# Moving the low part of h ahead of ez on GpSimd, and taking v's low weights last

## The chip, the cores and the metric

The kernel runs on one core of a Trainium2 chip, as one launch. The time is the device time of an execution in microseconds (us); lower is better. A core has a TensorE (PE; its weight loads are shown as PEld), a VectorE (DVE), a ScalarE (ACT), a GpSimd (POOL) and a SyncE (SP) that here only starts DMAs. Each engine works through its own list of instructions in order, and waits on semaphores for the others.

## The reference

Two blocks follow each other on x of 2048 tokens by 512 channels, in float32:

```python
h  = x + attention(layernorm(x))       # 32 heads of 16, linear attention
h2 = h + mixer(layernorm(h))           # MLP over the tokens, F = 1792
```

In the attention, q, k and v come from one product with `wqkv`. Each head's q and k go through a small product with `w_phi` and two softmaxes, of the logits and of their negatives; these are the features phi. With them `kv = phi_k^T v` and `z = sum phi_k` over all tokens, and the output is `phi_q kv / (phi_q z + 1e-6)`, times `wo`. The mixer normalises h per token, multiplies `w1` (2048 x 1792) over the token axis, adds `b1`, takes a tanh-gelu, multiplies `w2` (1792 x 2048) and adds `b2`.

## The kernel before

The tokens are cut into 16 tiles of 128 (`NT`). Every large product is made in three passes: each operand is split in a rounded high part and the low part that is left, and TensorE adds high x high, high x low and low x high in PSUM (`mm3`, lines 63 to 67). `split` (line 58) makes the two parts: ScalarE copies the high one (line 60), and another engine subtracts to get the low one (line 61).

**Preparation (lines 223 to 362).** The weights of q, k and v come in 12 chunks (0 to 3 q, 4 to 7 k, 8 to 11 v). They are centred (`center`), folded with w_phi or transposed on TensorE into PSUM (`fold`), and from there ScalarE writes the high parts (`hi_w`, line 285) and VectorE subtracts the low ones (`lo_w`, line 289). Chunks 10 and 11 of v lie in the two buffers of the PSUM pool `ps_v`; v's first product `v0` (line 335) takes the buffer that chunk 10 held. `proj` (lines 122 to 135) makes one product of a tile with 512 columns: 4 contraction steps of 3 matmuls. Its `by_part` form, used once for k's first tile, orders them by part of the weights instead. From line 294 on the order of TensorE, VectorE, ScalarE and GpSimd is written out by hand.

**k and v for all tiles, and q for six (lines 401 to 421).** Here the order on the engines is not written out; a planner that works on its own estimates of durations orders it when the kernel is built, and steps of this loop can also come between those written by hand. For each tile: k's product and its logits on VectorE, the exponential on ScalarE, the normalisation on GpSimd (`k_norm`), v's product; `kv` collects phi_k^T v in PSUM.

**Attention (lines 423 to 702).** From line 424 the order on the four engines is again written by hand. zB, the sum z spread over all partitions (lines 490 to 494), is copied by ScalarE from a product on TensorE, and starts GpSimd's work of this part. Then the loop `for it in range(NT + 4)` (line 648) works on several tiles at once, each at another step:

- `s_pq(it + 1)`: GpSimd multiplies a tile of features with its weights w (line 465);
- `s_num`, `s_ol`: the numerators of two tiles, every second iteration;
- `s_den`: VectorE's chain that starts with the sums of ez (line 456) and ends with w (line 462);
- `s_ez(it + 3)`: GpSimd multiplies a tile of exponentials with zB (line 447); `negate()` makes the negated logits there (lines 164 and 165);
- `fills(it)`: the first products of the mixer, for two column blocks of w1, block 0 with h tile it - 5 and block 1 with h tile it - 6. One such `fill` is six matmuls: for each half of the columns, high weights x high h (line 65), high weights x low h (line 66), low weights x high h (line 67);
- `q_exp`: an exponential of q on ScalarE (line 176), until iteration 7;
- `s_hn(it - 4)`: the normalised h tile, from r2 that GpSimd made with `s_rstd` (line 590) in the iteration before: three steps on ScalarE (lines 593, 595, 60) and the low part on GpSimd (line 61, shown as hs);
- `s_wo`, `s_tr`, `s_h`, `s_moments`: the product with wo, transposes, h itself and its statistics.

The weights of the mixer come in pairs of row tiles (`stream`, `fill_load`): a DMA, the high part on ScalarE (line 614), and later the low part on VectorE (`flush`, line 606). Pair 2 (rows of tiles 2 and 3) of block 0 is loaded at the end of iteration 5, its low part subtracted in iteration 6 and used in iteration 7; pair 2 of block 1 comes an iteration later each time.

**The rest of the mixer (lines 704 to 911)**: the remaining column blocks, gelu, and the second product (lines 823, 824 and 827). The change does not touch it.

Of the kernel before, what the change touches and what calls it, by code (L numbers as in the profile page):

```python
# [20 lines left out]
KD = D // P  # L21
# [15 lines left out]
def block_kernel(ctx: ExitStack, tc: tile.TileContext, x, xT, wT, phic, wo, w1, b1, w2, b2,  # L37
# [25 lines left out]
    def mm3(o, ah, al, bh, bl, first, last):  # L63

        nc.tensor.matmul(o, ah, bh, start=first, stop=False)  # L65
        nc.tensor.matmul(o, ah, bl, start=False, stop=False)  # L66
        nc.tensor.matmul(o, al, bh, start=False, stop=last)  # L67
# [22 lines left out]
    wvh = wp.tile([P, KD, D], F32R, name="wvh")  # L90
    wvl = wp.tile([P, KD, D], F32R, name="wvl")
    zacc = wp.tile([P, NG, P], F32, name="zacc")
    ps_k = a1.enter_context(tc.tile_pool(name="ps_k", bufs=2, space=PSUM))
    ps_v = a1.enter_context(tc.tile_pool(name="ps_v", bufs=2, space=PSUM))
# [24 lines left out]
        nc.vector.tensor_scalar(ve, st[:, 1:2], 1.0 / D, EPS, op0=ALU.mult, op1=ALU.add)  # L119
        nc.gpsimd.tensor_tensor(r1[:, t:t + 1], ve, mhalf[:, :1], op=ALU.pow)  # L120

    def proj(t, wh, wl, pool, name, by_part=False):
        o = pool.tile([P, D], F32, name=name, tag=name)
        if by_part:
            half, whole = [slice(0, D // 2), slice(D // 2, D)], slice(0, D)
            turn = [(0, wh, half[0]), (0, wh, half[1]), (1, wh, whole), (0, wl, half[0]), (0, wl, half[1])]
            for i, (a, w, cols) in enumerate(turn):
                for kt in range(KD):
                    nc.tensor.matmul(o[:, cols], X[t][:, a, kt, :], w[:, kt, cols], start=i == 0 and kt == 0,
                                     stop=i >= 3 and kt == KD - 1, skip_group_check=True)  # L130
            return o
        for kt in range(KD):
            mm3(o, X[t][:, 0, kt, :], X[t][:, 1, kt, :], wh[:, kt, :], wl[:, kt, :],
                kt == 0, kt == KD - 1)
        return o
# [39 lines left out]
    def exps(t, e):  # L175
        nc.scalar.activation(e, e, AF.Exp, scale=r1[:, t:t + 1])
# [46 lines left out]
    with tc.tile_pool(name="prep", bufs=1) as prep:  # L223
        pc = prep.tile([P, 72], F32, name="pc")
        ph = prep.tile([P, 4, P], F32, name="ph")
        WR = {}

        def load_w(c):
            if c % 2 == 0:
                pair = big.tile([P, 2, D], F32, name="wraw2", tag="big")  # L230
                WR[c], WR[c + 1] = pair[:, 0], pair[:, 1]
            nc.sync.dma_start(WR[c], wT[c * P:(c + 1) * P, :])

        nc.scalar.dma_start(pc, phic)
        for c in range(4, 8):
            load_w(c)
        xr = {0: load_x(0), 1: load_x(1)}
        nc.sync.dma_start(ident, ident_in)
        for c in range(8, 12):
            load_w(c)  # L240
        xr[2] = load_x(2)
        load_h(0)
        load_h(1)
        xr[3] = load_x(3)
        for c in range(4):
            load_w(c)
        load_h(2)
        xr[4] = load_x(4)
        load_h(3)
        nc.sync.dma_start(mask, kvmask)  # L250
        nc.sync.dma_start(b1s, b1)
        nc.sync.dma_start(b2s, b2)

        FO = {}
        HL = {0: (wqh, wql), 1: (wkh, wkl), 2: (wvh, wvl)}

        def center(c, vector):

            mu = prep.tile([P, 1], F32, name="mu", bufs=3)
            if vector:  # L260
                nc.vector.reduce_sum(mu, WR[c], axis=AX.X)
                nc.vector.tensor_scalar_mul(mu, mu, -1.0 / D)
                nc.vector.tensor_scalar(WR[c], WR[c], mu, None, op0=ALU.add)
            else:
                junk = prep.tile([P, D], F32, name="junk")
                nc.scalar.activation(junk, WR[c], AF.Copy, scale=-1.0 / D, accum_out=mu)
                nc.scalar.activation(WR[c], WR[c], AF.Identity, bias=mu)

        def fold(c, pool, name):
            FO[c] = pool.tile([P, KD, P], F32, name=name, tag=name)  # L270
            for kt in range(KD):
                if c < 8:
                    nc.tensor.matmul(FO[c][:, kt, :], WR[c][:, kt * P:(kt + 1) * P], ph[:, c % 4, :],
                                     start=True, stop=True)
                else:
                    nc.tensor.transpose(FO[c][:, kt, :], WR[c][:, kt * P:(kt + 1) * P], ident)

        def parts(c):
            return [w[:, :, c % 4 * P:(c % 4 + 1) * P] for w in HL[c // 4]]

        def hi_w(c, vector=False):
            if vector:
                nc.vector.tensor_copy(parts(c)[0], FO[c])
            else:
                nc.scalar.activation(parts(c)[0], FO[c], AF.Copy)

        def lo_w(c):
            hi, lo = parts(c)
            nc.vector.tensor_sub(lo, FO[c], hi)

        warm = ps_k.tile([P, P], F32, name="pk_ps", tag="pk_ps")
        for _ in range(WARM):
            nc.tensor.matmul(warm, ones, ones, start=True, stop=True)
        with tc.manual_schedule(engines={ET.PE, ET.DVE, ET.Activation, ET.Pool}):

            nc.gpsimd.tensor_mul(ph.rearrange("p c (a f) -> p c a f", f=DH),
                                 pc[:, 0:64].rearrange("p (c f) -> p c f", f=DH).unsqueeze(2).to_broadcast([P, 4, 8, DH]),
                                 pc[:, 64:72].unsqueeze(1).unsqueeze(3).to_broadcast([P, 4, 8, DH]))
            center(4, True)
            center(5, False)  # L300
            fold(4, ps_q, "pu")
            center(6, True)
            fold(5, ps_q, "pu")
            center(7, False)
            fold(6, ps_v, "pv")
            fold(7, ps_v, "pv")
            hi_w(4, True)
            hi_w(5, True)
            hi_w(6, True)
            split_x(0, xr[0])  # L310
            hi_w(7)
            for c in range(4, 8):
                lo_w(c)
            split_x(1, xr[1])
            k0 = proj(0, wkh, wkl, ps_k, "pk_ps", True)
            center(8, True)
            for c in range(9, 12):
                center(c, False)
            k1 = proj(1, wkh, wkl, ps_k, "pk_ps")
            for c in range(8, 12):  # L320
                fold(c, *((ps_q, "pu"), (ps_v, "pv"))[c // 10])
            k_ops(0, k0)
            split_x(2, xr[2])
            k_ops(1, k1)
            stats_x(0)
            k2 = proj(2, wkh, wkl, ps_k, "pk_ps")
            for c in range(8, 12):
                hi_w(c)
            for c in range(8, 12):
                lo_w(c)  # L330
            stats_x(1)
            exps(0, PK[0])
            split_x(3, xr[3])
            split_x(4, xr[4])
            v0 = proj(0, wvh, wvl, ps_v, "pv")
            k_ops(2, k2)
            stats_x(2)
            k3 = proj(3, wkh, wkl, ps_k, "pk_ps")
            k_norm(0)
            center(0, True)  # L340
            v_out(0, v0)
            exps(1, PK[1])
            center(1, False)
            exps(2, PK[2])
            v1 = proj(1, wvh, wvl, ps_v, "pv")
            k_ops(3, k3)
            fold(0, ps_q, "pu")
            fold(1, ps_q, "pu")
            k_norm(1)
            center(2, False)  # L350
            v_out(1, v1)
            hi_w(0)
            hi_w(1)
            lo_w(0)
            lo_w(1)
            center(3, False)
        stats_x(3)
        exps(3, PK[3])
        for c in range(2, 4):
            fold(c, ps_q, "pu")  # L360
            hi_w(c)
            lo_w(c)
# [208 lines left out]
    def s_x(t):  # L571
        HT[t] = ak.tile([P, D], F32, name="h", bufs=4)
        nc.sync.dma_start(HT[t], x[t * P:(t + 1) * P, :])
# [18 lines left out]
    def s_hn(t):  # L592
        nc.scalar.activation(VE[t][:, 1:2], VE[t][:, 1:2], AF.Copy, scale=r2[:, t:t + 1])
        hn = ak.tile([P, D], F32, name="hn")
        nc.scalar.activation(hn, HT[t], AF.Identity, scale=r2[:, t:t + 1], bias=VE[t][:, 1:2])
        HN[t] = big.tile([P, 2, D], F32R, name="hs", tag="big")
        split(HN[t][:, 0], HN[t][:, 1], hn, nc.gpsimd)
# [50 lines left out]
    for it in range(NT + 4):  # L648
        even = it % 2 == 0
# [15 lines left out]
            den = den[1:]  # L665
        if it < NT:
            s_x(it)
        if it + 3 < NT:
            s_ez(it + 3)
        negate()  # L670
# [1 line left out]
        fills(it)  # L672
        q_exp(0)
        logits = q_logits(1)
        if it >= 4 and even:
            s_hn(it - 4)
        if 3 <= it < NT + 3 and even:
            s_moments(it - 3)
        if it > 1 and even and it - 2 < NT:
# [161 lines left out]
    for n, (sp, p) in enumerate(STEPS):  # L841
        t = 2 * sp
# [5 lines left out]
        if p == 0:  # L848
            bank = []
            for _ in range(6):  # L850
                pool = (ps_f, ps_q, ps_b, ps_b)[n_bank % 8 // 2]
# [109 lines left out]
```

## Time and profile before

| what | value |
|---|---|
| time, median of 3 runs | 524.17 us (523.75 to 524.24) |
| the profiled execution's own time | 524.12 us |
| its span in the trace | 522.3 us |
| TensorE busy | 516.6 us, 99% |
| VectorE / ScalarE / GpSimd busy | 386.5 / 282.3 / 239.8 us |
| HBM traffic | 46.81 MB read, 11.14 MB written |

A row of the timeline gives start and duration in us, the engine, the line of the kernel, the operation, what it writes and reads by the program's names, the shapes, and a count of merged instructions; in brackets stands how long the engine was idle before it and what ended that. The rows of the sums by stretch give busy time (and number of instructions) of PE, PEld, DVE, ACT and POOL, the clock that TensorE was granted (1.00 is full), and what the DMA engines did. A waits row gives the total, the number of times and the longest one.

### The profile page before, as it was taken

The page shows a single profiled execution, that of the slowest core. Times are in us where ns is not written, and L with a number is a line of the kernel's source. Part 1 is how long each engine was busy: PE and PEld are TensorE (multiplying, and loading weights), DVE is VectorE, ACT ScalarE, POOL GpSimd, SP SyncE. Part 2 cuts the span into 40 slices and gives each one's busy share as a digit, 9 for nine tenths or more (in the row PEclk, how much of TensorE's full clock was granted, in tenths as well). Part 3 has the DMA queues.
Part 4 walks back from the last instruction along what each step waited for, and adds up shares of the span by engine and source line. Part 5 has one row for each costly group of instructions (what it writes and reads, how often), then busy time and mean ns, then how long its engine had stood idle before and what let it go on. Part 6 is the DMA issues. An engine that isn't in the chain of part 4 may idle for free.

```text
span 522.3 us, 8917 instructions
## 1 busy us (share of the span) xinstructions
PE 516.6 (99%) x3379; PEld 436.5 (84%) x3379; DVE 386.5 (74%) x681; ACT 282.3 (54%) x496; POOL 239.8 (46%) x188
## 2 busy tenths in 40 slices
PE   9999999999999999999999999999999999999997
PEld 8788888887877767888788888888899999999997
DVE  6893999986899998863227424725779888988985
ACT  6999853424246876666956423625453434434430
POOL 2579799985999999874424000000002112212220
PEclk9999999999999999999999999999999999999999
DMA  8544210020131324343333354532215687678734
GB/s 317 198 122 122 80 43 22 1 80 24 30 113 60 102 86 136 105 130 130 102 100 102 102 179 143 176 92 77 76 45 115 158 191 161 120 164 186 163 43 82
DMA packets 36298, 58.52 MB, mean 112 GB/s; under 512 B 3744, under 2 KB 19360, under 8 KB 36256
## 3 DMA queue, kind: packets, MB, share of 16 engines
q1 hardware_dynamic: 31936, 51.37, 31.2%
q0 software_dynamic: 4032, 6.42, 9.1%
q8 instruction: 26, 0.43, 0.3%
q10 hardware_dynamic: 288, 0.17, 0.1%
q14 instruction: 16, 0.13, 0.1%
HBM read 46.81 MB, written 11.14 MB: 111 GB/s over the span
## 4 chain that ended last, share of the span: by engine, by line
PE 90%; POOL 7%; DVE 2%; issue 1%; ACT 0%; POOLq 0%
PE pu L65 12%; PE pu L66 12%; PE pu L67 11%; PE py L823 11%; PE py L827 10%; PE py L824 6%; PE pv L66 3%; PE pv L67 3%; PE pv L65 3%; PE pk_ps L65 2%; PE pk_ps L67 2%; PE pk_ps L66 2%; POOL ez L447 2%; POOL eq L465 2%; PE po L67 2%; PE po L65 2%
## 5 line engine op out<-in xcount | busy, mean ns | idle before, releaser
L66 PE MATMUL pu<-hs,whi 128*128 128x512 f32 x224 | 87.6, 391 | 1.2 <-POOL hs L61 1.2
L65 PE MATMUL pu<-hs,whi 128*128 128x512 f32 x224 | 87.4, 395 | 0.0
L67 PE MATMUL pu<-hs,wlo 128*128 128x512 f32 x224 | 87.0, 389 | 0.0
L606 DVE TENSOR_TENSOR wlo<-wraw,whi 128x512 fp32r<-128x512 f32 x56 | 43.8, 784 | 53.2 <-ACT whi L614 53.0
L882 POOL DMA_DIRECT2D out<-ot x7 | 6.2, 887 | 153.9 <-DVE ot L878 153.9
L796 ACT ACTIVATE whi<-wraw 128x1792 fp32r<-128x1792 f32 x28 | 47.4, 1701 | 46.7 <-PE py L823 20.6
L805 DVE TENSOR_TENSOR wlo<-wraw,whi 128x1792 fp32r<-128x1792 f32 x28 | 56.5, 2022 | 12.1 <-PE py L824 8.9
L823 PE MATMUL py<-uf,whi 128*128 128x512 f32 x175 | 63.4, 399 | 0.0
L614 ACT ACTIVATE whi<-wraw 128x512 fp32r<-128x512 f32 x56 | 34.9, 627 | 49.6 <-PE pu L66 45.3
L65 PEld LDWEIGHTS pu<-hs,whi 128*128 128x128 f32 x224 | 42.1, 188 | 10.9 <-issue 2.5
L66 PEld LDWEIGHTS pu<-hs,whi 128*128 128x128 f32 x224 | 42.1, 188 | 10.4 <-POOL hs L61 2.1
L67 PEld LDWEIGHTS pu<-hs,wlo 128*128 128x128 f32 x224 | 42.1, 188 | 8.6
L824 PE MATMUL py<-uf,wlo 128*128 128x256 f32 x175 | 49.2, 281 | 0.0
L447 POOL TENSOR_TENSOR ez<-eq,zB 128x1024 f32<-128x1024 f32 x16 | 38.4, 2400 | 4.4 <-ACT zB L494 4.4
L827 PE MATMUL py<-uf,whi 128*128 128x256 f32 x210 | 39.0, 283 | 0.0
L823 PEld LDWEIGHTS py<-uf,whi 128*128 128x128 f32 x175 | 33.0, 188 | 6.8
L200 POOL TENSOR_TENSOR pk<-pk,sk 128x1024 f32<-128x1024 f32 x16 | 31.0, 1940 | 7.6 <-DVE sk L199 5.0
L534 ACT ACTIVATE pht<-tn 128x512 f32<-128x512 f32 x32 | 17.4, 596 | 30.2 <-PE tn L532 30.2
L827 PEld LDWEIGHTS py<-uf,whi 128*128 128x128 f32 x210 | 32.4, 189 | 1.4
L824 PEld LDWEIGHTS py<-uf,wlo 128*128 128x128 f32 x175 | 33.1, 189 | 0.0
L465 POOL TENSOR_TENSOR eq<-eq,w 128x1024 f32<-128x1024 f32 x16 | 32.3, 2017 | 1.3 <-DVE w L462 1.2
L61 POOL TENSOR_TENSOR hs<-hn,hs 128x512 fp32r<-128x512 f32 x16 | 21.6, 1350 | 23.7 <-ACT hs L60 23.7
(179 smaller groups left out, 1344.2 us busy)
## 6 DMA issues: line engine op xcount, KB each, us to landing
wraw<-in_w SPq DMA_DIRECT2D x56, 256.0 KB, 2.8
wraw<-in_w SPq DMA_DIRECT2D x28, 512.0 KB, 4.1
xraw<-in_xT SPq DMA_DIRECT2D x16, 256.0 KB, 2.8
xh<-in_x SPq DMA_DIRECT2D x16, 256.0 KB, 2.6
h<-in_x SPq DMA_DIRECT2D x16, 256.0 KB, 2.7
out<-h SPq DMA_DIRECT2D x16, 256.0 KB, 2.4
out<-ot POOLq DMA_DIRECT2D x14, 256.0 KB, 4.8
wraw<-in_wT SPq DMA_DIRECT2D x12, 256.0 KB, 4.4
```

Source lines behind the costliest of these rows:

```text
L65: nc.tensor.matmul(o, ah, bh, start=first, stop=False)
L66: nc.tensor.matmul(o, ah, bl, start=False, stop=False)
L67: nc.tensor.matmul(o, al, bh, start=False, stop=last)
L447: nc.gpsimd.tensor_mul(EZ[t], EQ[t], zB)
L465: nc.gpsimd.tensor_mul(heads(EQ[t]), heads(EQ[t]), W[t].rearrange("p g c h -> p (g c h)").unsqueeze(2).to_broadcast([P, 2 * H, DH]))
L606: LO.append(nc.vector.tensor_sub(wl_, raw, wh_).ins)
L614: nc.scalar.activation(wh_, raw, AF.Copy)
L796: nc.scalar.activation(WH[g], RAW[g], AF.Copy)
L805: nc.vector.tensor_sub(wl_, RAW[g], WH[g])
L823: nc.tensor.matmul(o, a[0], b, start=start, stop=stop, skip_group_check=True)
L824: nc.tensor.matmul(o[:, 0], a[1], b[:, 0], start=False, stop=stop, skip_group_check=True)
L827: nc.tensor.matmul(o[:, half], a[x], b[:, y], start=start and first and i == 0, stop=stop and i == 2, skip_group_check=True)
```

## The change

It has two parts. In the preparation, v's first product goes through the four contraction steps with high x by high weights, then low x by high weights, then high x by low weights; and VectorE subtracts the low parts of v's weight chunks in the order 10, 11, 8, 9. In the attention loop, `s_hn(it - 4)` of the even iterations from 4 on stands ahead of `s_ez(it + 3)`, instead of behind `q_logits`. On GpSimd it thus passes ez and the first `negate()`, on ScalarE what `fills` may issue there and the exponential of `q_exp`. The odd iterations stay as they are.

```diff
-    def proj(t, wh, wl, pool, name, by_part=False):
+    def proj(t, wh, wl, pool, name, by_part=False, low_last=False):
         o = pool.tile([P, D], F32, name=name, tag=name)
-        if by_part:
+        if by_part or low_last:
             half, whole = [slice(0, D // 2), slice(D // 2, D)], slice(0, D)
             turn = [(0, wh, half[0]), (0, wh, half[1]), (1, wh, whole), (0, wl, half[0]), (0, wl, half[1])]
+            if low_last:
+                turn = [(0, wh, whole), (1, wh, whole), (0, wl, whole)]
             for i, (a, w, cols) in enumerate(turn):
                 for kt in range(KD):
                     nc.tensor.matmul(o[:, cols], X[t][:, a, kt, :], w[:, kt, cols], start=i == 0 and kt == 0,
-                                     stop=i >= 3 and kt == KD - 1, skip_group_check=True)
+                                     stop=w is wl and kt == KD - 1, skip_group_check=True)
             return o
...
-            for c in range(8, 12):
+            for c in (10, 11, 8, 9):
                 lo_w(c)
...
-            v0 = proj(0, wvh, wvl, ps_v, "pv")
+            v0 = proj(0, wvh, wvl, ps_v, "pv", low_last=True)
...
         if it < NT:
             s_x(it)
+        if it >= 4 and even:
+            s_hn(it - 4)
         if it + 3 < NT:
             s_ez(it + 3)
         negate()
...
         logits = q_logits(1)
-        if it >= 4 and even:
-            s_hn(it - 4)
         if 3 <= it < NT + 3 and even:
```

## The prediction

> **What bounds the kernel now.** The order of reading is: the page's busy times, the sums by stretch, the waits, then the timeline at the places that these name. The first row below is the page's, the others are sums by stretch: between 23.3 us and the end TensorE is busy without a break, except between 172 and 190 us.
>
> ```profile
> PE 516.6 (99%) x3379; PEld 436.5 (84%) x3379; DVE 386.5 (74%) x681; ACT 282.3 (54%) x496; POOL 239.8 (46%) x188
> ```
> ```profile
> 23.30:172.00 148.70, 148.70 (x1214) 121.81 (x1213) 127.63 (x229) 86.32 (x154) 129.72 (x89) 1.00 0.22 67
> ...
> 190.00:519.00 329.00, 329.00 (x1937) 282.59 (x1934) 222.54 (x380) 163.10 (x277) 84.50 (x75) 1.00 0.48 122
> ```
>
> So a microsecond is won only where TensorE stands still, and lost wherever a new wait stops it. Next come the view of waits and TensorE's timeline at the one stop of size after the warm-up.
>
> ```profile
> PE pu L66 <- POOL hs L61: 1.2, 1, 1.2
> ```
> ```profile
> 186.68 0.39 PE L67 MATMUL pu<-hs,wlo 128*128 128x512 f32 x1
> 186.91 0.39 PE L65 MATMUL pu<-hs,whi 128*128 128x512 f32 x1
> 188.46 0.50 PE L66 MATMUL pu<-hs,whi 128*128 128x512 f32 x1 [1.16 <-POOL hs L61]
> 188.80 0.40 PE L67 MATMUL pu<-hs,wlo 128*128 128x512 f32 x1
> ```
>
> The records of matmuls overlap, so their starts say more: one of 128x512 starts every 0.23 us (186.68, 186.91). In iteration 7 the product with the low part of h tile 2 starts 1.55 us after the one before it, so 1.32 us are lost. The next one follows at 0.34 instead of 0.23: each stop costs about 0.1 us more in restarting.
>
> The second stop stands too briefly in each piece for the view of waits; the starts show it.
>
> ```profile
> 19.63 0.39 PE L67 MATMUL pk_ps<-wkh,xs 128*128 128x512 f32 x1
> 20.06 0.47 PE L65 MATMUL pv<-wvh,xs 128*128 128x512 f32 x1
> 20.56 0.50 PE L66 MATMUL pv<-wvl,xs 128*128 128x512 f32 x1
> 20.91 0.40 PE L67 MATMUL pv<-wvh,xs 128*128 128x512 f32 x1
> ...
> 23.68 0.39 PE L67 MATMUL pk_ps<-wkh,xs 128*128 128x512 f32 x1
> ```
>
> Here k's third product starts its last matmul at 19.63, v's first product follows at 20.06, 20.56 and 20.91, where 0.23 apart would be 19.86, 20.09, 20.31. With the slow steps behind them (15 steps of 0.23 after 19.63 give 23.08 for the row at 23.68) it is 0.60 us.
>
> **Part 1: v's first product.** VectorE's low-weight subtractions, ScalarE's high parts of chunks 10 and 11, and GpSimd's low part of x tile 3:
>
> ```profile
> 18.04 1.28 DVE L289 TENSOR_TENSOR wvl<-pu,wvh 128x512 fp32r<-128x512 f32 x2
> 19.23 1.28 DVE L289 TENSOR_TENSOR wvl<-pv,wvh 128x512 fp32r<-128x512 f32 x2
> ...
> 24.30 0.15 DVE L119 TENSOR_SCALAR ve<-st 128x1 f32<-128x1 f32 x1 [1.34 <-ACT sqj L117]
> ```
> ```profile
> 17.58 1.09 ACT L285 ACTIVATE wvh<-pv 128x512 fp32r<-128x512 f32 x2
> ```
> ```profile
> 21.76 1.30 POOL L61 TENSOR_TENSOR xs<-xraw,xs 128x512 fp32r<-128x512 f32 x1 [0.56 <-ACT xs L60]
> ```
>
> The 12 matmuls and 12 weight loads of the product stay, at the same width; only their order changes, so they cost nothing themselves. Before, the first waits for a PSUM buffer that the third subtraction frees (19.23 + 0.68 = 19.91), the second for the fourth subtraction (19.23 + 1.28 = 20.51).
>
> After, chunk 10 goes first on VectorE. It needs its high part, which ends near 18.2, so VectorE loses 0.1 to 0.2 us, hidden by its idle 1.34 us at 24.30. The buffer is free by 18.9, before TensorE comes at 19.86. The low weights are asked for only by the ninth matmul, 8 x 0.23 later at 21.70, and are done near 20.7. So the whole 0.60 us goes. What is late next: the third matmul of k's fourth product would come at 23.08, and its operand, the low part of x tile 3, ends on GpSimd at 21.76 + 1.30 = 23.06, some 0.05 too late with the 0.06 us from an operand's end to its matmul (186.69 + 1.72 = 188.41 to 188.46, in part 2). ScalarE and GpSimd don't move there. With a restart of 0.1 to 0.15 (as at 20.91), 0.4 of the 0.60 us is kept; ends 0.3 and 0.6.
>
> Is it kept to the end? These are steps on GpSimd around the start of its dense stretch.
>
> ```profile
> 123.03 1.35 POOL L165 TENSOR_TENSOR eq<-mn,eq 128x512 f32<-128x512 f32 x1 [0.41 <-DVE eq L150]
> 128.82 2.40 POOL L447 TENSOR_TENSOR ez<-eq,zB 128x1024 f32<-128x1024 f32 x1 [4.43 <-ACT zB L494]
> ```
>
> To 126 us TensorE has no break, so nothing else sets its pace. GpSimd's dense stretch then begins by waiting 4.43 us for zB (at 128.82), which ScalarE copies from a TensorE product; so what GpSimd and VectorE do from there moves with TensorE, and I take the 0.4 through to the end.
>
> **Part 2: the low part ahead of ez.** In the even iterations 4 to 12 three ScalarE instructions and one on GpSimd move; from 14 on there is no ez left to pass. No DMA is issued by the step; the load of h rows on SP waits for a buffer that it frees, which comes earlier, not later. These are ScalarE's and GpSimd's steps in iteration 6.
>
> ```profile
> 180.60 1.15 ACT L176 ACTIVATE eq<-eq,r 128x1024 f32<-128x1024 f32 x1
> 181.64 0.29 ACT L593 ACTIVATE ve<-ve,r 128x1 f32<-128x1 f32 x1
> 181.96 0.82 ACT L595 ACTIVATE hn<-h,ve,r 128x512 f32<-128x512 f32 x1
> 182.81 0.63 ACT L60 ACTIVATE hs<-hn 128x512 fp32r<-128x512 f32 x1
> ```
> ```profile
> 180.57 0.55 POOL L590 TENSOR_TENSOR r<-ve,mhalf 128x1 f32<-128x1 f32 x1
> ...
> 184.34 2.38 POOL L447 TENSOR_TENSOR ez<-eq,zB 128x1024 f32<-128x1024 f32 x1
> 186.69 1.72 POOL L61 TENSOR_TENSOR hs<-hn,hs 128x512 fp32r<-128x512 f32 x1
> ```
>
> On ScalarE it passes an exp of 1.15 us in iterations 4 and 6. In iteration 6 it must then wait for r2, which GpSimd has at 180.57 + 0.55 = 181.12; then 0.29 + 0.82 + 0.63 us put the high part at about 183.0. It had ended at 182.81 + 0.63 = 183.44.
>
> GpSimd comes free at 184.34, so the low part of h tile 2 runs 184.34 to 185.6 (1.24 from start to start when nothing disturbs it) instead of ending at 188.40 (186.69 + 1.72). ez follows, 185.6 to 187.96 instead of to 186.72. TensorE's 1.32 us stop at h is gone.
>
> What is late next is another operand of the same product: the low half of weight pair 2 of the first column block (c, at 186.22 below), which VectorE subtracts. The rows are all of VectorE's low weights, three of them, and GpSimd beside the later two (d and e).
>
> ```profile
> L606 DVE TENSOR_TENSOR wlo<-wraw,whi x56: 677/694/2220, 166.1 to 369.3; 128x512 fp32r<-128x512 f32 x56
> ```
> ```profile
> 186.22 1.05 DVE L606 TENSOR_TENSOR wlo<-wraw,whi 128x512 fp32r<-128x512 f32 x1
> ...
> 191.50 2.22 DVE L606 TENSOR_TENSOR wlo<-wraw,whi 128x512 fp32r<-128x512 f32 x1
> ...
> 193.65 0.68 DVE L606 TENSOR_TENSOR wlo<-wraw,whi 128x512 fp32r<-128x512 f32 x1
> ```
> ```profile
> 190.77 2.41 POOL L447 TENSOR_TENSOR ez<-eq,zB 128x1024 f32<-128x1024 f32 x1
> 193.67 1.81 POOL L61 TENSOR_TENSOR hs<-hn,hs 128x512 fp32r<-128x512 f32 x1 [0.49 <-ACT hs L60]
> ```
>
> Before, c ended at 187.27, and a matmul without the stop would ask for it at 187.37. Why does it take 1.05 us when the median is 0.69? Because GpSimd was in ez until 186.72; it ended 0.55 after that. The pair at 191.50 (d) shows it without doubt: 2.22 us, ending 193.72, 0.55 after the ez that runs until 193.18.
>
> So this subtraction cannot run beside a GpSimd operation that started before it. With ez now running to 187.96, c ends at 188.51, and its matmul starts at 188.57 instead of 188.80: 0.23 won, 0.1 given back by the second restart, 0.13 in all. If the port cost nothing the gain would be 1.3.
>
> The Trainium skill ("SBUF — State Buffer", section "SBUF: two separate sides") says that VectorE, in an operation with two SBUF inputs, and GpSimd take one port pair as an exclusive lock for the whole instruction. By that rule c waits out ez and the gain is the 0.13; the trace agrees (2.22 against 0.69).
>
> One step on, in iteration 8, TensorE asks for the low half e of the second column block's pair 2. Its matmul, and VectorE's rows beside GpSimd's 123.03 above:
>
> ```profile
> 195.07 0.39 PE L67 MATMUL pu<-hs,wlo 128*128 128x512 f32 x1
> ```
> ```profile
> 122.78 0.68 DVE L485 TENSOR_TENSOR zacc<-zacc,pk 128x512 f32<-128x512 f32 x1
> ...
> 123.38 1.55 DVE L485 TENSOR_TENSOR zacc<-zacc,pk 128x512 f32<-128x512 f32 x1
> ```
>
> Before, e was issued at 193.65, before d's record ended, and the low part of h tile 3 just behind it at 193.67, so e went first and GpSimd's operation grew to 1.81. After: GpSimd comes free for the steps up to the next ez at 188.51, when c ends, instead of at 188.40, so d ends at 193.73 to 193.83 and e is issued at 193.66 to 193.76; but h tile 3 follows TensorE's transposes through ScalarE and comes 0.13 earlier, at 193.54. Who goes first is shown once: at 123.03 GpSimd is issued while VectorE holds the port, VectorE's next one at 123.38 waits for it (1.55 instead of 0.68).
>
> So h tile 3 goes first, ends 1.15 after d (as before after e, which ended at 194.33) at 194.88 at the earliest, and e 0.55 later at 195.43. TensorE would ask at 194.94 and starts at 195.49: 0.55 lost and 0.1 for the restart. Ends of this term: 0 and 0.65.
>
> The rest costs nothing. The reader of ez in iteration 5, as an example:
>
> ```profile
> 175.73 1.20 DVE L456 TENSOR_REDUCE tz<-ez 128x64 f32<-128x1024 f32 x1
> ```
>
> By the order in the code it lies a whole iteration behind that ez, and ez comes 1.24 us later, the time of the low part. Without that cover VectorE would start this sum later, and TensorE needs its result only an iteration on. From iteration 7 on TensorE leaves GpSimd idle between its steps (0.49 us at 193.67), and by the code all later weight pairs are subtracted a whole iteration before they are asked for.
>
> **The sum.** -0.4 - 0.13 + 0.65 = +0.1 us on the profiled execution's 524.12 (0.05 under the median 524.17): 524.2.
>
> **The rivals.** (B) e still goes before h tile 3. For it: they were 0.02 us apart. Against: h gains 0.13. Then -0.4 - 0.13: 523.6. (C) The stop is won whole, because c slips in ahead of ez or its subtraction doesn't meet it: -0.4 - 1.3 - 0.1 (no restart either) on 524.12: 522.3. It needs VectorE 0.65 us earlier against GpSimd than before, or ez started after 186.22; against it, both chains hang on TensorE and move together.
>
> (D) Slower. VectorE, and TensorE's first matmul of a later k product:
>
> ```profile
> 51.04 0.15 DVE L119 TENSOR_SCALAR ve<-st 128x1 f32<-128x1 f32 x1 [2.71 <-POOL r L120]
> ...
> 57.44 0.68 DVE L154 TENSOR_TENSOR pk<-mn,pk_ps 128x512 f32<-128x512 f32 x1
> ```
> ```profile
> 61.63 0.39 PE L65 MATMUL pk_ps<-wkh,xs 128*128 128x512 f32 x1
> ```
>
> The loop at lines 404 to 421 is ordered by a planner, and v's first product ends earlier in its plan. VectorE already stands 2.71 us before one tiny statistics step there (51.04), with k products waiting in PSUM behind it. TensorE takes a k buffer again at 61.63, 3.5 us after VectorE leaves it (57.44 + 0.68 = 58.12). A new order that puts two more such waits ahead of the k products makes VectorE 5.4 late and stops TensorE for 1.9, which swallows the 0.4: 526.0. It decides from 3.5 us of lateness. Against it: every plan has the same work, and TensorE has no stop there now.
>
> **How the numbers follow.** Forecast 0.33, B 0.15, C 0.26, D 0.26 (0.03 of it with a loss that stays small). A measurement of this kernel can tell about 0.2%, 1.05 us. Faster beyond that: C, 0.26. Within: forecast, B and the small D, 0.51. Slower: 0.23. The range reaches from C most of the way to D, 522.2 to 525.4, leaving out half of D and little below; the forecast's own is 523.5 to 524.8.
>
> **What would show it.** Part 1: v's first product starting at 19.86 and running at 0.23 us, and a short stop at the third matmul of the next product. Part 2: no wait for h near 187 us, but the third matmul with h tile 2 waiting for VectorE's low weights, whose record is near 2.3 us long; then, in iteration 8, the same again for e if h tile 3 went first. Wrong it would be if that c record is short, if TensorE stops between 30 and 126 us, or if the plan's order there is another.

## The result

The changed kernel takes 524.74 us (median of 22 executions, 524.36 to 525.69); the kernel before, run beside it, 523.96 us (median of 22, 523.54 to 525.63). The ratio is 1.0015, with a 95% interval of 1.0009 to 1.0021: the change costs 0.8 us (0.5 to 1.1), inside the 0.2% that the prediction took for the limit of a measurement. The forecast was 524.2 us.

The profiled execution of after took 525.69 us with a span of 523.9 us. It is the longest of its 22, and 1 us of it does not belong to the change. The waits of TensorE in it, then ScalarE at the load of a weight chunk in after and in before:

```profile
PE pu L67 <- DVE wlo L608: 1.5, 2, 1.0
PE pk_ps L295 <- DVE eps L56: 1.1, 1, 1.1
PE pv L275 <- ACT wraw L269: 1.0, 1, 1.0
...
```
```profile
7.78 0.63 ACT L268 ACTIVATE junk<-wraw 128x512 f32<-128x512 f32 x1 [1.96 <-DMA wraw<-in_wT]
```
```profile
5.93 0.63 ACT L266 ACTIVATE junk<-wraw 128x512 f32<-128x512 f32 x1 [0.28 <-DMA wraw<-in_wT]
```

A line of the program stands two higher in after (L608 is the low weights, L606 before). The third wait, 1.0 us at the folds, is a chunk whose load landed late: ScalarE waited 1.96 us for it instead of 0.28, before any instruction that the change touches. At the fiftieth matmul after is 0.99 us behind before; in the profiles of the experiments below the same place lies between 0.47 ahead and 0.44 behind. So the traces are compared by how the distance between matmuls of equal number grows from there, not by their ends. (The 525.69 us less this 0.99 are 524.70, close to the median of 524.74.)

**The attention.** The wait for h tile 2 (1.2 us in the view of before) is gone, and TensorE waits twice for VectorE's low weights. As in the prediction, c and e are the low weights of pair 2 of the first and of the second column block, and d are those that VectorE subtracts just ahead of e. TensorE's timeline, VectorE's and GpSimd's at both places:

```profile
188.18 0.39 PE L66 MATMUL pu<-hs,whi 128*128 128x512 f32 x1
189.59 0.50 PE L67 MATMUL pu<-hs,wlo 128*128 128x512 f32 x1 [1.03 <-DVE wlo L608]
...
195.69 0.40 PE L66 MATMUL pu<-hs,whi 128*128 128x512 f32 x1
196.51 0.50 PE L67 MATMUL pu<-hs,wlo 128*128 128x512 f32 x1 [0.42 <-DVE wlo L608]
196.85 0.40 PE L65 MATMUL pu<-hs,whi 128*128 128x512 f32 x1
```
```profile
187.23 2.31 DVE L608 TENSOR_TENSOR wlo<-wraw,whi 128x512 fp32r<-128x512 f32 x1
...
193.78 0.98 DVE L608 TENSOR_TENSOR wlo<-wraw,whi 128x512 fp32r<-128x512 f32 x1
...
194.68 1.77 DVE L608 TENSOR_TENSOR wlo<-wraw,whi 128x512 fp32r<-128x512 f32 x1
```
```profile
185.35 1.28 POOL L61 TENSOR_TENSOR hs<-hn,hs 128x512 fp32r<-128x512 f32 x1
186.59 2.39 POOL L449 TENSOR_TENSOR ez<-eq,zB 128x1024 f32<-128x1024 f32 x1
...
191.81 2.39 POOL L449 TENSOR_TENSOR ez<-eq,zB 128x1024 f32<-128x1024 f32 x1
194.56 1.34 POOL L61 TENSOR_TENSOR hs<-hn,hs 128x512 fp32r<-128x512 f32 x1 [0.35 <-ACT hs L60]
```

The low part of h tile 2 (185.35) now ends before TensorE wants it. Low weights c are issued at 187.23, while ez runs until 188.98, and end 0.56 behind it: 2.31 us for work of 0.69. Their matmul comes at 189.59 (188.80 before). In iteration 8 d ends at 194.76 and the low part of h tile 3 is issued at 194.56, ahead of e at 194.68; so e ends at 196.45, and its matmul comes at 196.51 (195.07 before).

**Part 1.** TensorE at v's first product and k's fourth, in after, and the first matmul behind the fourth product's short stop in before:

```profile
20.85 1.98 PE L131 MATMUL pv<-wvh,xs 128*128 128x512 f32 x8
22.66 1.07 PE L131 MATMUL pv<-wvl,xs 128*128 128x512 f32 x4
...
23.80 0.39 PE L66 MATMUL pk_ps<-wkl,xs 128*128 128x512 f32 x1
24.10 0.50 PE L67 MATMUL pk_ps<-wkh,xs 128*128 128x512 f32 x1
24.44 0.39 PE L65 MATMUL pk_ps<-wkh,xs 128*128 128x512 f32 x1
```
```profile
23.91 0.39 PE L65 MATMUL pk_ps<-wkh,xs 128*128 128x512 f32 x1
```

v's twelve matmuls start 0.227 us apart (20.85 to 22.66 are eight steps), and the next product's third matmul comes 0.07 late (0.30 after 23.80) and costs a restart (0.34). At 24.44 after is 0.53 behind before, where it had been 0.99 behind: 0.46 us won. Thirty microseconds on they are lost again, without a wait in any view. TensorE in before and in after:

```profile
48.60 0.39 PE L67 MATMUL pv<-wvh,xs 128*128 128x512 f32 x1
48.92 0.30 PE L212 MATMUL kvp<-pk,vs 128*32 128x64 f32 x2
49.15 0.50 PE L66 MATMUL pu<-wql,xs 128*128 128x512 f32 x1
49.49 0.39 PE L67 MATMUL pu<-wqh,xs 128*128 128x512 f32 x1
...
53.79 0.50 PE L65 MATMUL pu<-wqh,xs 128*128 128x512 f32 x1
```
```profile
48.95 0.39 PE L67 MATMUL pv<-wvh,xs 128*128 128x512 f32 x1
49.27 0.30 PE L214 MATMUL kvp<-pk,vs 128*32 128x64 f32 x2
49.50 0.49 PE L65 MATMUL pu<-wqh,xs 128*128 128x512 f32 x1
49.92 0.30 PE L214 MATMUL kvp<-pk,vs 128*32 128x64 f32 x4
50.16 0.50 PE L66 MATMUL pu<-wql,xs 128*128 128x512 f32 x1
50.49 0.40 PE L67 MATMUL pu<-wqh,xs 128*128 128x512 f32 x1
...
54.78 0.50 PE L65 MATMUL pu<-wqh,xs 128*128 128x512 f32 x1
```

In before, one short piece of the kv matmuls stands ahead of q's product's second matmul; from 48.60 to 49.49 pass 0.89 us, where two steps of 0.227 are 0.45. In after there are two pieces, and 48.95 to 50.49 are 1.54 us where three steps are 0.68. So a piece costs about 0.4 us, and the planner, whose order of this loop the change moved, put in a second one. At the first large matmul behind the kv group (54.78 against 53.79) after is 0.99 us behind again. No view names this: TensorE counts as busy through it, for 27.00 of the 27.00 us from 30 to 57 us in both traces.

### The profile page after: what moved, and what is told of

It reads as the page before. It is cut to its first block, busy times and chain, and to the rows that moved or that the text cites. A ratio compares the mean times of both kernels' runs of the same rounds, so it can differ in the third digit from the quotient of the medians.

```text
span 523.9 us, 8916 instructions
## 1 busy us (share of the span) xinstructions
PE 516.7 (99%) x3379; PEld 436.1 (83%) x3379; DVE 389.3 (74%) x681; ACT 282.1 (54%) x496; POOL 239.8 (46%) x188
## 4 chain that ended last, share of the span: by engine, by line
PE 94%; DVE 3%; ACT 1%; DMA 1%; issue 0%; SPq 0%; DVEq 0%; ACTq 0%
PE pu L65 12%; PE pu L67 12%; PE pu L66 12%; PE py L825 11%; PE py L829 10%; PE py L826 6%; PE pk_ps L65 3%; PE pk_ps L67 3%; PE pk_ps L66 3%; PE pv L65 3%; PE pv L66 3%; PE pv L67 3%; PE tn L534 2%; PE po L67 2%; PE po L65 2%; PE po L66 2%
## 5 line engine op out<-in xcount | busy, mean ns | idle before, releaser
L608 DVE TENSOR_TENSOR wlo<-wraw,whi 128x512 fp32r<-128x512 f32 x56 | 46.3, 830 | 53.3 <-ACT whi L616 53.0
```

What stands on the lines that cost most here:

```text
L608: LO.append(nc.vector.tensor_sub(wl_, raw, wh_).ins)
```

## The experiments

All are measured against the kernel before on the same chip; the interval of a ratio is about 0.001, 0.5 us, so the times are read together with the traces. The "distance" is again that of matmuls of equal number from the profile of before; it is negative where the run is ahead of before. Most runs have ten or eleven executions, p2_half and best2 only five.

| run | time, us | before, us | ratio (95% interval) |
|---|---|---|---|
| p1: part 1 alone | 523.93 | 523.77 | 0.9999 (0.9990 to 1.0008) |
| p1_pin: part 1, kv behind q's first product | 523.15 | 523.77 | 0.9986 (0.9977 to 0.9995) |
| before_pin: the kernel before, kv behind q's first product | 523.46 | 523.97 | 0.9992 (0.9983 to 1.0001) |
| p2: part 2 alone | 524.44 | 523.77 | 1.0009 (1.0001 to 1.0018) |
| p2_early: part 2, c subtracted early | 524.53 | 523.77 | 1.0009 (1.0000 to 1.0018) |
| p2_swap: part 2, e ahead of d | 524.12 | 523.82 | 1.0002 (0.9993 to 1.0011) |
| p2_early_swap: both | 523.00 | 523.82 | 0.9984 (0.9975 to 0.9994) |
| p2_half: part 2, one ez in halves | 525.96 | 523.82 | 1.0032 (1.0019 to 1.0045) |
| best2: p1_pin with p2_early_swap | 522.01 | 523.82 | 0.9964 (0.9952 to 0.9977) |

### Part 1 alone

The kernel of after, with `s_hn` of the even iterations back behind `q_logits`.

> Part 1 alone. In the profile of the whole change part 1 was won at k's fourth product (its last matmul 0.46 us sooner) and lost again between 30 and 57 us, where the plan of the loop has another order. Theory (the new order costs TensorE a second short kv piece inside q's first product, 0.45 us of changes between the two kinds of matmul): 0.0 against before, -0.15 to +0.15. Rival (that loss comes from elsewhere, from the late load at the start of that one execution): -0.45.

Measured: no difference (523.93 against 523.77). In the trace the distance goes from -0.14 to -0.58 at k's fourth product and back to -0.15 behind the kv group; TensorE's order here is that of after, with both pieces. So part 1 wins its 0.44 and the plan takes 0.43 of it back.

### Part 1 without the pieces, and the kernel before without its own

```diff
-            for t in range(v - 4, v):
-                kv(t)
+            with tc.issue_after(END["pu"]) if v == 4 else ExitStack():
+                for t in range(v - 4, v):
+                    kv(t)
```

`END["pu"]` is the last matmul of q's first product; `mm3` returns it. The block is queued behind it on TensorE.

> Part 1 with the first four tiles' kv matmuls queued behind q's first product, so that no short kv piece stands inside it. Theory (pieces cost): the 0.45 of part 1 is kept, and before's own single piece near 48.9 us goes too (some 0.3 to 0.4): -0.45 to -0.85 against before, with k's fourth product, the folds and the kv groups free of stops. Rival (the new order costs through something else, VectorE or the folds): 0.0, as part 1 alone.

Measured: -0.62 us (-0.3 to -1.2). TensorE around the kv group in p1_pin:

```profile
52.03 0.39 PE L67 MATMUL pu<-wqh,xs 128*128 128x512 f32 x1
52.35 1.99 PE L214 MATMUL kvp<-pk,vs 128*32 128x64 f32 x128
54.27 0.50 PE L65 MATMUL pu<-wqh,xs 128*128 128x512 f32 x1
```

The 128 kv matmuls stand together. At k's fourth product the distance falls by 0.42, and over the kv group by another 0.44. The same edit in the kernel before, with nothing of the change:

> The kernel before, with nothing of the change, but with the first four tiles' kv matmuls queued behind q's first product: the price of a short kv piece by itself. Theory (the one piece that stands inside q's product near 48.9 us costs 0.44, as the starts around it say): -0.4 against before (-0.3 to -0.5), stops at h tile 2 and at v's first product unchanged. Rival (a piece costs nothing, and the plan's order gained elsewhere): 0.0.

Measured: -0.51 us (-0.9 to +0.05; an interval that just reaches no change). In the trace the distance goes from -0.46 at 48.60 to -0.91 behind the kv group, and stays there: the one piece of before costs 0.45. Traces with none, one and two pieces thus differ by the price of one piece each. In the pinned kernels q's and v's 128x512 matmuls still alternate, at steps of 0.23 us, so it is not the change from one product to another that costs.

### Part 2 alone

The kernel of after, with v's first product and the order of the low weights as before.

> Part 2 alone. Theory (the subtraction of low weights c waits out ez, and the one of e goes behind the low part of h tile 3): +0.6 against before (+0.4 to +0.7), both stops at the low weights as in the whole change. Rival B (e goes first once part 1 is not there): -0.1. Rival C: -1.3.

Measured: +0.67 us (0.05 to 0.9). In the trace +0.58 is added between 172 us and 197 us, with the same two stops at the low weights. The order of the planned loop is that of before here, with one kv piece, so the second piece comes with part 1. The loss of the whole change is part 2's.

### The first stop taken away

```diff
+        if it == 6:
+            flush()
         if it > 1 and even and it <= NT:
             ol = s_ol(it // 2 - 1)
```

> Part 2, and in iteration 6 low weights c subtracted at the head of VectorE's list instead of behind the chain of den, so that ez cannot hold it up: the first stop (1.3 us with its restart) is gone. Theory (GpSimd's chain of ez, r2, pq, ez, h tile 3 sets the pace here; d, h tile 3 and e come at the same times, and TensorE, there sooner, waits for e as much longer): the stop at e grows from 0.6 to about 2 us, and the time is that of part 2 alone, +0.3 to +0.7. Rival (the two stops are independent): -0.75 against before.

Measured: 524.53 us, the time of part 2 alone (524.44), though a stop of 1.2 us is gone. TensorE, VectorE and GpSimd in iteration 8 of p2_early:

```profile
193.94 0.40 PE L66 MATMUL pu<-hs,whi 128*128 128x512 f32 x1
195.63 0.50 PE L67 MATMUL pu<-hs,wlo 128*128 128x512 f32 x1 [1.30 <-DVE wlo L608]
```
```profile
191.73 2.17 DVE L608 TENSOR_TENSOR wlo<-wraw,whi 128x512 fp32r<-128x512 f32 x1
...
193.82 1.75 DVE L608 TENSOR_TENSOR wlo<-wraw,whi 128x512 fp32r<-128x512 f32 x1
```
```profile
193.30 1.73 POOL L61 TENSOR_TENSOR hs<-hn,hs 128x512 fp32r<-128x512 f32 x1
```

c is subtracted at 181.43 and holds nobody up. But d (191.73) and e (193.82) stand behind an ez and the low part of h tile 3 that come when GpSimd's own row of work lets them, so e ends at 195.57 however early TensorE is there. The stop at e is 1.69 us from start to start, 1.47 above a step, where it was 0.59 above in p2. What was won at c was waited away one iteration later: the first stop was worth nothing while the second stood behind it.

### e ahead of d, without and with the early c

```diff
-        for p in range(2):
+        for p in (1, 0) if it == 6 else (0, 1):
             if it >= LAG - 3 + p and FL[p] <= FN[p] + 2 * (FN[p] > 0):
                 fill_load(p)
```

> Part 2, and at the end of iteration 6 the pair of block 1 (e) loaded, and so subtracted, ahead of the pair of block 0 (d). Theory (VectorE and GpSimd take turns in the order in which they ask: d stood first, h tile 3 second, e third): now e is first, h tile 3 second, in time for its own matmul 1.6 us later, and d, which is wanted an iteration on, last. The stop at e goes, the one at c stays: 0.0 to -0.2 against before. Rival (h tile 3, now behind e, is late instead): +0.6, as part 2 alone.

Measured: +0.3 us, no difference that can be told (-0.4 to +0.6). In the trace the stop at e is gone and the one at c is kept (1.1 us of waiting), as expected, and from 172 us to the end the distance changes by -0.09 in all: -0.11 at h tile 0, +0.13 at h tile 1, -0.10 at c, which comes that much sooner than h tile 2 did. Against part 2 alone (+0.58 there) the order of e and d is worth 0.67.

> Part 2 with both: c subtracted at the head of iteration 6, and e ahead of d. Theory (the early c was worth nothing only because e came at a time that GpSimd's chain sets): with e first it ends near 193.9, ahead of its matmul at 194.2, and h tile 3 near 195.05 ahead of its own at 195.2, so that no stop is left in iterations 7 and 8: -1.3 to -1.5 against before. Rival (GpSimd's chain itself is the bound, the next operand is late instead, h tile 3): 0 to -0.5.

Measured: -0.82 us (-1.3 to -0.3). TensorE, VectorE's e and GpSimd in p2_early_swap:

```profile
193.89 0.40 PE L66 MATMUL pu<-hs,whi 128*128 128x512 f32 x1
194.12 0.40 PE L67 MATMUL pu<-hs,wlo 128*128 128x512 f32 x1
...
195.28 0.39 PE L66 MATMUL pu<-hs,whi 128*128 128x512 f32 x1
```
```profile
191.74 2.18 DVE L608 TENSOR_TENSOR wlo<-wraw,whi 128x512 fp32r<-128x512 f32 x1
```
```profile
193.32 1.75 POOL L61 TENSOR_TENSOR hs<-hn,hs 128x512 fp32r<-128x512 f32 x1
```

e ends at 193.92 and its matmul runs at 194.12 with no wait; h tile 3 is done at 195.07 and the first matmul with its low part runs at 195.28. No wait for h or for low weights is left in the view. The early c, which gave nothing while e came late (+0.46 in p2_early's trace against +0.58 in p2's), gives 0.95 once e is out of the way (-1.04 against -0.09). The trace wins 1.04 from 172 us on, 0.3 less than expected: a stop that was not foreseen, at TensorE's product with wo in iteration 6 (0.16 us and 0.11 of restart), where the numerators' low part now stands behind c on VectorE, and 0.09 at the product with wo near 197 us.

### One ez in two halves

```diff
-        nc.gpsimd.tensor_mul(EZ[t], EQ[t], zB)
+        n = 4 if t == 9 else NG
+        for g in range(0, NG, n):
+            nc.gpsimd.tensor_mul(EZ[t][:, g:g + n], EQ[t][:, g:g + n], zB[:, g:g + n])
```

> Part 2 with the ez of iteration 6 as two operations of half the size. Theory (c waits for the end of the GpSimd operation that runs when it is issued, and goes ahead of the next): c ends 0.55 after the first half, its record is 1.0 to 1.2 us long instead of 2.3, and the first stop is gone but for 0.1 to 0.2; ez, r2, pq, ez and h tile 3 come some 0.6 later behind c, and the stop at e grows to over 2 us, so that the time is +0.9 to +1.4 against before. Rival (the stops are independent): -0.5. Rival for the port (c waits for all of ez, not for one operation): c's record stays at 2.3 and the time at +0.6.

Measured: +2.1 us (1.0 to 2.4), more than any theory had. VectorE's c and GpSimd's two halves, then TensorE at the second stop and behind it, and the sums by stretch there:

```profile
185.77 1.20 DVE L610 TENSOR_TENSOR wlo<-wraw,whi 128x512 fp32r<-128x512 f32 x1
```
```profile
185.11 3.01 POOL L451 TENSOR_TENSOR ez<-eq,zB 128x512 f32<-128x512 f32 x2
```
```profile
195.18 0.50 PE L67 MATMUL pu<-hs,wlo 128*128 128x512 f32 x1 [1.66 <-DVE wlo L610]
...
196.70 0.63 PE L66 MATMUL pu<-hs,whi 128*128 128x512 f32 x1
197.13 0.63 PE L67 MATMUL pu<-hs,wlo 128*128 128x512 f32 x1
```
```profile
193.30:195.20 1.90, 0.24 (x2) 0.02 (x1) 1.90 (x3) 1.37 (x3) 1.90 (x2) 1.00 0.37 89
...
196.00:197.00 1.00, 1.00 (x4) 0.81 (x3) 1.00 (x2) 0.97 (x2) 1.00 (x1) 0.58 0.51 95
197.00:198.00 1.00, 1.00 (x4) 0.72 (x4) 1.00 (x3) 0.97 (x3) 0.99 (x2) 0.50 0.97 357
```

For the port it came out as the theory says: c went between the halves, 1.20 us long instead of 2.31, and the first stop shrank to 0.12. The stop at e grew to 2.06 from start to start, 1.83 above a step, as expected. Behind it the granted clock (the third number from the right) fell to 0.50: from about 196.2 us (the 0.58 of the first slice) to 199.6 us a matmul starts every 0.43 us (196.70, 197.13) instead of 0.23, which costs some 1.6 us more. The five executions of this kernel took 524.48, 525.33, 525.96, 525.99 and 526.00 us, and the last three have a mean clock of 0.996 where the other two have 1.000 and 0.999. The trace grows by 0.76 from 172 us to where the clock falls, and the execution at 524.48 lies 0.66 above before. So without the clock the kernel stands at about +0.7, just under the theory's +0.9, and in the traced execution the clock is the rest. Why one execution took 525.33 with a clock of 0.999 is not known; it has no trace.

### Both parts without their losses

Part 1 with the kv matmuls kept together, part 2 with the early c and e ahead of d: best2.

> Part 1 with the kv matmuls queued behind q's first product, and part 2 with c early and e ahead of d. If the terms add, -0.6 of the first and -1.3 to -1.5 of the second: -1.9 to -2.1 against before. If the first part's gain is given back at GpSimd's chain in the attention: -1.3 to -1.5.

Measured: 522.01 us against 523.82, -1.8 us (-1.2 to -2.5); it beats both kernels. All of TensorE's waits in best2:

```profile
PE pk_ps L295 <- DVE eps L56: 1.1, 1, 1.1
PE pu L275 <- DVE wraw L265: 0.4, 1, 0.4
PE pk_ps L131 <- ACT wkh L287: 0.2, 1, 0.2
```

They are those of the start alone. In the trace part 1 with the kv group gives -0.82 and the attention -1.08, and neither is given back at the other: the terms add. As in p2_early_swap, the attention gives some 0.3 less than the 1.3 to 1.5 expected; here it goes in small stops near 192.5 and 195.3 us, 0.28 together.

## Why the prediction was right, and where it was not

The forecast of 524.2 us was a sum of about nothing, and the time is 0.5 us above it, within its range and, by 0.06 us, its own narrower one. Part of that is luck: the kernel before took 523.96 us this time instead of 524.17, its median ahead of the forecast, and the difference between the kernels, which the sum put at +0.1, is +0.8. Of its two halves one was right term by term, and the other was right at its place and wrong further on. From the trace of after:

| term | forecast, us | measured, us |
|---|---|---|
| part 1 at k's fourth product | -0.4 | -0.46 |
| part 1 "through to the end" | kept | +0.46, lost at the kv pieces |
| c instead of h tile 2 | -0.23 | -0.23 |
| restart behind c | +0.1 | +0.10 |
| e behind the low part of h tile 3 | +0.55 | +0.55 |
| restart behind e | +0.1 | +0.11 |
| h tile 0 and h tile 1 | 0 | -0.11 and +0.14 |
| sum | +0.1 | +0.56 |

The whole distance grows by 0.61; the last 0.05 go in steps that are each too small to name.

**Part 2** went as written: the operand next behind h tile 2, the port that c waits for, its end 0.55 behind ez, the order in which d, h tile 3 and e are served, and both prices. The experiments that undo one cause each (p2_early, p2_swap, p2_half) moved the stop that they were aimed at. Two things were not in the sum: TensorE had a short stop at h tile 0 (0.11) that goes, and one at h tile 1 (0.13 above a step in before) that grew to 0.25 in iteration 6. The two belong together: GpSimd ends the low part of h tile 1 at 180.61 us in before and at 181.63 in after, 1.02 later and so no sooner than the 0.99 by which after is behind, and TensorE waited away there what it had won at h tile 0. Rival C fails since c met ez, and rival B since h tile 3 was 0.12 us ahead of e.

**Part 1** failed at the step "Is it kept to the end?". It reasoned that TensorE has no break up to 126 us, so nothing else sets its pace, and that what is won early therefore stays. That takes TensorE's own list as given. But the list between the two hand-written stretches is the planner's, and with part 1 in its plan the planner put a second short kv piece into q's first product. Which of part 1's two edits moved the plan, and by which of its estimates, is not shown. Rival D had the right place and the right agent, the new order of that loop, but looked for the loss in VectorE's lateness and a stop of TensorE from 3.5 us on; what came is a cost of TensorE's own order, 0.4 us for each short piece, with no stop at all. Its argument against, "every plan has the same work, and TensorE has no stop there now", was the blind spot: a busy engine can be a slower one. The piece in before (48.92) was in the trace to be seen, and its price with it.

The half that failed makes up the difference of 0.46 between the forecast's +0.1 and the +0.56 of the rows; the medians' +0.8 (0.5 to 1.1) agrees with the latter.

## What to carry to other kernels

A wait removed at one operand is worth only the distance to the next operand that comes late, and when several of them hang on one busy engine, as on GpSimd here, the last in the chain has to go for the first to count: in the traces the early c gave 0.12 us alone, e ahead of d 0.67 alone, and both together 1.62. When a hand-written stretch is followed by one that a planner orders, read how its order comes out anew, since a gain ahead of it can be spent inside it without a wait in any view; pin the pieces that should stay together. An engine that is 99% busy is still to be read by the distance of its starts.

## What the runs showed of the hardware

**A stop of under 2 us of waiting can halve TensorE's clock.** In p2_half the gap is 2.06 us (193.12 to 195.18) with 1.66 us of waiting, and the granted clock was 0.50 from about 196.2 to 199.6 us. In p2_early a gap of 1.69 us with 1.30 us of waiting left it at 1.00:

```profile
195.60:197.00 1.40, 1.37 (x6) 1.15 (x7) 1.40 (x4) 0.95 (x2) 1.40 (x2) 1.00 0.51 126
```

By the Trainium skill ("TensorE: Matmul & The Clock Gate", section "What's actually happening") the clock falls after at least one idle window of about 3.4 us, and the windows run freely, so that it depends on where in one the work lies. The length of the slow time here, 3.4 us, agrees with such a window, and so does that three of five executions show a lower mean clock; the threshold does not, since here some 1.7 us of waiting were enough. Only one of these executions has a trace.

The traces' record of the clock bears the windows out: in p2_half the full clock stands from 5.01 to 196.16 us, which is 56 times 3.413 us, and again from 199.57, one such time on; in the other ten traces it stands for 151 or 152 times 3.413 us (515.4 or 518.8). Counted in these steps from 5.39 us, where p2_early's full clock begins, the stop of p2_early lies whole inside the window from 193.12 to 196.53, as that of p2_half does inside its own from 192.75 to 196.16. So where the stop lies in a window does not tell the two apart, and the limit for this mix of work lies between 1.3 and 1.7 us of waiting in one window, as far as two traces can show it.

**A change between large and small matmuls has a price.** A step from a 128x512 matmul to a short run of the 128x64 ones and back costs some 0.4 us above the steps themselves: 0.45 in before_pin, where one piece goes, 0.43 in p1, where one comes. The cost shows in the starts alone. What about the small matmuls makes it (their size, or that they use 32 columns) is not shown.

**The port goes to who asks first.** With d running, h tile 3 at 194.56 was served ahead of e at 194.68 in after; in before e, at 193.65, was served ahead of h tile 3 at 193.67; and in p2_half c, issued at 185.77, went between the two halves of ez. Each waiting subtraction of low weights ended 0.55 to 0.56 us behind the GpSimd operation that it waited for.
